# Joining the k and v products of two units, two output slots, and another order of the last stores, in a linear-attention and ELU-MLP kernel

## The chip, the core and the metric

The kernel runs on one core of one Trainium2 chip. It is one launch, and its time is the device time of that core in microseconds. A time given for a kernel is the median of several executions; a profile is one more execution, recorded by the hardware profiler. The engines of the core run their own lists of instructions and wait for one another through semaphores: TensorE (PE, with PEld for its weight loads), VectorE (DVE), ScalarE (ACT), GpSimd (POOL) and SyncE (SP). SP, ACT and POOL can also issue DMA transfers.

## The reference

Per head, q is normalised by a softmax over its 64 features, k by a softmax over the sequence. The product of k and v is a 64x64 matrix per head; q times that matrix is the attention output. Rows of 512 features (8 heads) then go through two dense layers with an ELU between.

```python
def _attn_ref(q, k, v):                       # 8 batches, 8 heads, 576 rows, 64 features
    q_s = softmax(q, axis=-1)
    k_s = softmax(k, axis=2)
    kv = np.einsum('bhsd,bhse->bhde', k_s, v)
    return np.einsum('bhsd,bhde->bhse', q_s, kv)

def _moe_ref(x, w_in, w_out):                 # x 4608x512, w_in 512x2048, w_out 2048x512
    h = x @ w_in
    g = np.where(h > 0.0, h, np.exp(np.minimum(h, 0.0)) - 1.0)
    return g @ w_out
```

(The softmaxes are written out in the reference; they are shortened here.)

## The kernel before

**Attention.** A unit is half of the heads of one batch element, so there are 16 units, two per batch element, numbered 0 to 15. For a unit, q and k are loaded as 128x1152 tiles (`QR`, `KR`) and v as `VR`. `stage1` takes the exponential of q and k on ScalarE (L397, L427 for units 0 and 1, whose q goes in two halves; L401), casts v to bf16 with a column of ones behind it (`VB`, L414 and L417), sums q's exponentials (L429), takes reciprocals (L432) and scales q (`QS`, L440). q is transposed by TensorE for units 0 to 3 (`tp`, L464, copied out at L471 and L474 into `qsT`), and by a transposing DMA from SP for the others (`turn`, L480, widened at L490 or L492).

`kv_mm` (L520) forms the product of k and v: 36 matmuls on 64x64 quarters of the array, 65 columns each, because the column of ones gives the sum of k's exponentials as well. `m` (L529, L533) is VectorE's scaling of that product into `MBLK`. `ao_mm` (L551) and, for units 0 and 1, `ao_parts` (L563) multiply the transposed q by `MBLK`: the attention output, two matmuls of up to 512 columns. `xt` (L585, L588) copies it into `XT`, the ring of rows for the dense layers.

A TensorE group is what `side` (L495) makes: several of these parts issued as one step that owns both halves of one accumulation tile. From unit 4 on the tile is always the same one (`AB`, two banks). A unit's attention output comes in two groups (part 0 and part 1). `batch(b)` (L1010) emits, for the units n = 2b and n+1, the q work and four such groups, and hangs the k/v products of the next batch's units on them: that of unit n+2 on part 0 of unit n+1, that of unit n+3 on its part 1. Those of units 4 and 5 are groups of their own.

The v cast has two tiles, but `VB1` lies over a region that is needed later, so `vb` (L366) uses it for units 1 and 3 only; from unit 4 on all casts go to the one tile `VB0`, and a cast waits until the last product has read it.

**Dense layers.** The 4608 rows are 9 blocks of 512, j = 0 to 8. For each block and each of 8 groups g, `hg_mm` (L636) makes 256 hidden features with 8 matmuls of 512 columns. `hg` follows with ScalarE's exponential (L652, into `ESB`), a second ScalarE step (L672) or a VectorE one (L680), and VectorE's combination into `GR` (L675, L682).

Blocks 0 and 1 go through the second layer plainly (`out_mm`, L697; `out_store`, L715). From block 2 on, `pair` (L819) computes two row tiles of 128 rows at once with seven products of half matrices instead of eight, on sums and differences of `GR` that GpSimd makes (`sums` and `late`, L797) and on combinations of w_out made once (`combos`, L768). A pair has four steps. Its four quarters live in two banks, H[0] to H[3]. ScalarE copies a quarter out (`copy`, L871), VectorE adds others on (`dve`, L866), and the results are in two row tiles: X (halves XL, XR) and Y. Y is complete in the third step, X in the fourth. `store` (L722) sends a row tile out as two DMAs of 64 rows, which L730 issues. Blocks 2 to 5 do a quarter of the second layer plainly within the pair (`std`, L858); blocks 6 to 8 (`WHOLE` and up) do all of it with half matrices and are called full.

X and Y of the pairs are slots `OSB0` to `OSB2`: X alternates between slots 0 and 2 (`self.pairs`), Y is always slot 1; the very last pair puts Y into `ESB0`. A slot can be written again only when the DMAs that read it have landed.

**Order.** Every operation is an entry that `Sched.add` records, with what it reads (R), writes (W), or holds exclusively (X); from this `emit` derives the semaphore waits. In which order an engine runs its entries is written out by hand: `ORDER` holds for each engine the list of entry numbers. The second argument of `add` is an assumed duration. It has no part in the order on an engine; it places the entries of all engines in one sequence for emission and sets how many filler matmuls (L948, on a unit matrix) `fill` puts into TensorE's early waits.

Entries of the start that the lists name: 22 and 38 are the exponentials of k of units 0 and 1; 25 and 29 those of q's halves of unit 0, 41 and 45 of unit 1; 23 and 39 ScalarE's v casts; 34 and 36 copies of the transposed q of unit 0; 37 and 60 the k/v products of units 0 and 1; 44 a scaling of q of unit 1 and 52 its five transposes; 49 to 51 the scaling of unit 0's product; 56 and 57 the attention output of unit 0, 58 and 59 its copies; 64 and 65 that of unit 1; 78 and on the hidden-layer matmuls of block 0.

## Time and profile before

| | us |
|---|---|
| median of three executions | 297.68 (297.46 to 297.81) |
| profiled execution, its own time | 297.21 |
| span of the profiled execution | 295.4 |
| exponentials of the hidden layer, ScalarE L652, 72 of them | 73.8 busy |
| matmuls of the hidden layer, L636, 576 of them | 142.8 busy |
| mean clock granted to TensorE, share of full | 0.998 |

The span runs from the first to the last recorded instruction; 1.8 us of the time lie outside it. Busy time of an engine counts each moment once. A row of the timeline gives start, length, engine, line of the kernel, operation, output and input, the number of instructions merged into the row, and, in brackets, how long the engine had stood idle before and what ended that. A merged row of matmuls is as long as from its first start to its last end, and as matmuls overlap, distances between starts say more than lengths. DMA rows are the issue on a queue; the transfer lands later.

### The profile page before, as it was taken

The numbers are of one execution on the slowest core, as the hardware profiler recorded it, in microseconds if no ns is written. First come the engines' busy times: TensorE is split into PE (matmuls) and PEld (weight loads), VectorE is DVE, ScalarE is ACT, GpSimd is POOL, SyncE is SP. The second block draws the span as 40 slices with busy tenths as digits, with TensorE's granted clock in tenths as the row PEclk, the third lists the DMA queues.
The fourth block names the chain that finished last, engine by engine and source line by source line (L and its number), as shares of the span: only waits on it lengthen the run. The fifth ranks groups of instructions, "written<-read, shape, count | busy, mean of one in ns | idle before, by whom it ended". The sixth has DMA issues, their size and how long they took to land.

```text
span 295.4 us, 5358 instructions
## 1 busy us (share of the span) xinstructions
PE 284.8 (96%) x2129; PEld 242.6 (82%) x2129; DVE 176.8 (60%) x326; ACT 210.9 (71%) x249; POOL 221.1 (75%) x216
## 2 busy tenths in 40 slices
PE   2999999999999999999999999999999999999993
PEld 0588777778888889888888888888889998988993
DVE  3849925786644667566656756755445366365653
ACT  5758838979998797986887596875874576666610
POOL 2990365343689998998798778799679967899870
PEclk9999999999999999999999999999999999999999
DMA  7999998899795544767849481404203110301315
GB/s 267 400 363 390 387 389 323 216 276 338 206 277 140 145 155 84 243 106 272 240 120 277 132 244 31 93 2 93 57 0 71 38 36 2 71 13 26 71 36 144
DMA packets 36473, 50.03 MB, mean 169 GB/s; under 512 B 16352, under 2 KB 18144, under 8 KB 36448
## 3 DMA queue, kind: packets, MB, share of 16 engines
q1 hardware_dynamic: 29760, 34.09, 41.4%
q0 software_dynamic: 6528, 15.47, 17.4%
q8 instruction: 17, 0.28, 0.4%
q10 hardware_dynamic: 160, 0.13, 0.2%
q14 instruction: 8, 0.07, 0.1%
HBM read 36.70 MB, written 9.44 MB: 156 GB/s over the span
## 4 chain that ended last, share of the span: by engine, by line
PE 91%; POOL 2%; ACT 2%; DVE 1%; DMA 1%; issue 0%; POOLq 0%
PE PS L636 44%; PE PS L845 24%; PE PS L697 9%; PE PS L858 5%; PE PS L551 3%; PE PS L520 2%; POOL GR L797 2%; PE PS L948 2%; DMA QR<-in_q_dram 1%; PE PS L464 1%; DVE GR L675 1%; DVE OSB L866 1%; PE PS L563 0%; ACT qsT L471 0%; ACT ESB L672 0%
## 5 line engine op out<-in xcount | busy, mean ns | idle before, releaser
L636 PE MATMUL PS<-XT,W 128*128 128x512 f32 x576 | 142.8, 392 | 0.0
L636 PEld LDWEIGHTS PS<-XT,W 128*128 128x128 f32 x576 | 104.7, 188 | 20.6 <-ACT OSBX L715 0.4
L675 DVE SCALAR_TENSOR_TENSOR GR<-PS,ESB 128x512 fp32r<-128x512 f32 (+1 forms) x124 | 87.4, 706 | 54.4 <-ACT ESB L672 52.4
L652 ACT ACTIVATE ESB<-PS 128x1024 f32<-128x1024 f32 x72 | 73.8, 1027 | 44.9 <-PE PS L636 43.8
L672 ACT ACTIVATE ESB<-ESB 128x1024 f32<-128x1024 f32 x64 | 67.9, 1060 | 1.4
L797 POOL TENSOR_TENSOR GR<-GR 128x512 fp32r<-128x512 f32 (+1 forms) x65 | 62.9, 980 | 5.1 <-PE PS L845 3.9
L866 DVE TENSOR_TENSOR OSB<-OSB,PS 128x256 f32<-128x256 f32 x83 | 34.5, 416 | 35.2 <-PE PS L845 34.5
L845 PE MATMUL PS<-W,GR 128*128 128x256 f32 x288 | 46.0, 284 | 0.3 <-POOL GR L797 0.3
L440 POOL TENSOR_TENSOR QS<-QR,RZQ 128x1152 f16<-128x1152 f32 (+1 forms) x16 | 30.3, 1895 | 20.3 <-DVE RZQ L432 19.7
L845 PE MATMUL PS<-TB,GR 128*128 128x256 f32 x288 | 43.5, 283 | 0.0
L845 PEld LDWEIGHTS PS<-W,GR 128*128 128x128 f32 x288 | 40.7, 191 | 2.5 <-POOL GR L797 0.5
L845 PEld LDWEIGHTS PS<-TB,GR 128*128 128x128 f32 x288 | 39.7, 190 | 1.7
L797 POOL TENSOR_TENSOR SB<-GR 128x256 fp32r<-128x256 f32 (+1 forms) x31 | 30.1, 975 | 13.5 <-DVE GR L675 11.8
L697 PE MATMUL PS<-W,GR 128*128 128x512 f32 x128 | 33.1, 398 | 0.0
L797 POOL TENSOR_TENSOR GR<-SB,GR 128x256 fp32r<-128x256 f32 (+1 forms) x31 | 29.9, 980 | 2.7 <-PE PS L845 2.2
L417 POOL CAST VB<-VR 128x1152 bf16<-128x1152 f32 (+1 forms) x16 | 18.0, 1122 | 14.5 <-DMA VR<-in_v_dram 9.8
L697 PEld LDWEIGHTS PS<-W,GR 128*128 128x128 f32 x128 | 23.2, 188 | 4.9 <-DMA W<-in_moe_w_out_dram 0.3
L585 ACT ACTIVATE XT<-PS 128x512 fp32r<-128x512 f32 (+6 forms) x32 | 19.2, 605 | 9.9 <-PE PS L551 5.8
L429 DVE TENSOR_REDUCE ZQ<-QR 128x18 f32<-128x1152 f32 (+2 forms) x18 | 21.7, 1206 | 6.0 <-ACT QR L427 4.2
L401 ACT ACTIVATE KR<-KR 128x1152 bf16<-128x1152 f32 x16 | 18.4, 1159 | 1.2 <-DMA KR<-in_k_dram 1.2
L858 PE MATMUL PS<-W,GR 128*128 128x512 f32 x64 | 17.6, 396 | 0.0
L871 ACT ACTIVATE OSB<-PS 128x256 f32<-128x256 f32 x27 | 10.1, 380 | 9.8 <-PE PS L845 7.5
(59 smaller groups left out, 223.0 us busy)
## 6 DMA issues: line engine op xcount, KB each, us to landing
out_dram<-OSB SPq DMA_DIRECT2D x60, 128.0 KB, 2.4
QR<-in_q_dram SPq DMA_DIRECT2D x12, 576.0 KB, 4.8
KR<-in_k_dram SPq DMA_DIRECT2D x12, 576.0 KB, 5.1
VR<-in_v_dram SPq DMA_DIRECT2D x12, 576.0 KB, 5.4
W<-in_moe_w_out_dram POOLq DMA_DIRECT2D x4, 1024.0 KB, 16.8
QR<-in_q_dram POOLq DMA_DIRECT2D x4, 576.0 KB, 9.3
KR<-in_k_dram POOLq DMA_DIRECT2D x4, 576.0 KB, 13.0
VR<-in_v_dram POOLq DMA_DIRECT2D x4, 576.0 KB, 12.9
```

The source lines that it names most:

```text
L429: S.add("dve", t_dve(m), lambda e, qp=qp, zp=zp: e.tensor_reduce(zp, qp, AX.X, ALU.add), key - 3, R=[f"qR{i}{x}" for x in xs], W=[f"ZQ{i}{ ...
L440: lambda e, qp=q[:, :, a:b, :], rz=rz, dst=qs[:, :, a:b, :]: e.tensor_tensor(dst, qp, rz, ALU.mult),
L585: S.add("act", t_act((h1 - h0) * n_, True), lambda e, dst=dst, src=src: e.activation(dst, src, AF.Copy), key, W=W, X=X)
L636: last = e.matmul(P[:, t * 512:(t + 1) * 512], self.W1[:, kc, tt * 128:(tt + 1) * 128], self.XT[:, kc, rc:rc + BLK], start=(kc == 0), stop ...
L652: S.add("act", t_act(1024, True), lambda e: e.activation(esb[:, :], self.PS[ps][:, :], AF.Exp), key, W=[f"E{i}"], X=banks)
L672: S.add("act", t_act(1024, False), lambda e: e.activation(esb[:, :], esb[:, :], AF.Relu, bias=1.0, scale=-1.0), key, X=[f"E{i}"])
L675: S.add("dve", t_dve(512 if j else 1024), lambda e, u=u: e.scalar_tensor_tensor(*(x[:, :, u, :] if j else x for x in (gt, P)), 0.0, ev[:, ...
L697: last = e.matmul(dst, self.tile(jb, jj, ts), self.W2[:, jj, c0:c1], start=(jj == 0), stop=(jj == 15))
L797: lambda e: e.tensor_tensor(dst, a, b, op), key, R=R, W=W, X=X, after=after)
L845: last = e.matmul(dst, a[i][:, y_, :], b[i][:, y_, :], start=start and i == 0 and y_ == 0, stop=stop and i == len(grps) - 1 and y_ == z - ...
L858: last = e.matmul(self.bank(bk), self.tile(j, jj, 2 * ts + p), self.W2[:, jj, :], start=False, stop=stop and jj == jj1 - 1, skip_group_che ...
L866: S.add("dve", t_dve(256), lambda e: e.tensor_tensor(dst, a, b, ALU.add), key, R=R, W=W, X=X, after=after)
```

## The change

- The k/v products of units n+2 and n+3 are parts of one group: both hang on part 1 of unit n+1, in neighbouring columns. Units 4 and 5 have one group for both (`kv2`). Assumed durations 615 and 350 become 505 and 305.
- The bf16 tile of v alternates for all units; `VB1` has memory of its own.
- Two slots `OSB0` and `OSB1` are allocated, and three more (`OSB2` to `OSB4`) lie over the raw q and k tiles. Pairs of blocks 2 to 5 use slots 0 and 1, X and Y changing places from pair to pair. Full pairs use slots 0 and 1 for the first pair of a block and 2 and 3 for the second.
- In the last pair the right half of the last row tile goes into slot 4, is finished in the third step, before the last matmuls, and is stored then; the left half is finished and stored after them.
- Of the last block's second row tile, the second half of the rows goes out on ScalarE's queue (the condition names block 8 and row tile 1).
- All five lists of `ORDER` are replaced. With one entry fewer from the group of units 4 and 5 on, entry numbers there stand one lower than before.

The core of the diff, with those pieces of the lists that are spoken of:

```diff
 ORDER = {
     "pe": (
-        "35 54 33 37 52 56 57 60 78 80 79 64 65 83 81 84 87 82 85 88 86 89 99 103 110 133 121 107 "
+        "35 54 33 37 57 56 52 60 78 80 79 64 65 82 81 84 87 85 88 83 86 89 99 103 110 121 107 133 "
...
-        "999 1021 1022 1055 1027 1028 1056 1023 1029 1057 1052 1010 1053 1031 1037 1054 1079 1080 "
-        "1038 1081 1039 1043 1113 1064 1084 1090 1085 1117 1091 1086 1073 1092 1114 1118 1094 "
+        "1056 991 1017 1051 1052 1009 1053 1078 1030 1026 1079 1020 1083 1021 1042 1022 1027 1028 "
+        "1080 1084 1063 1036 1037 1089 1090 1091 1112 1085 1038 1072 1113 1093 1099 1100 1116 "
...
-        "1294 1288 1289 1295 1290 1267 1268 1269 1282 1283 1284 1304 1305 1298 1299 1300 1306 "
-        "1309 1310 1311 1315 1316 1317 "),
+        "1294 1266 1267 1268 1281 1282 1287 1283 1288 1289 1303 1304 1305 1297 1298 1299 1311 "
+        "1312 1313 1317 1318 1319 "),
     "act": (
-        "3 29 25 45 41 22 23 36 34 38 39 58 53 66 90 93 94 96 100 101 104 111 112 114 122 108 134 "
+        "3 29 45 25 22 41 23 36 38 34 39 58 53 66 90 93 94 96 100 101 104 111 112 122 108 137 114 "
...
     "dve": (
-        "4 2 5 6 0 7 30 31 46 47 26 27 42 28 43 44 49 50 51 59 55 61 62 63 67 91 92 95 97 98 102 "
+        "4 2 5 6 0 7 30 31 46 47 26 27 28 42 43 49 50 51 44 59 55 61 62 63 67 91 92 95 97 98 102 "
...
     "sp": (
...
-        "420 333 424 489 556 530 546 531 432 438 557 545 567 439 623 572 622 638 568 637 586 679 "
+        "418 419 489 488 530 529 555 438 544 545 556 437 428 622 621 566 567 637 573 636 678 703 "
...
-        "1172 1234 1235 1286 1287 1303 1302 1313 1314 1319 1322 "),
+        "1233 1234 1218 1286 1285 1308 1301 1302 1315 1321 "),
...
-        self.OSB = [a(f"OSB{i}", [128, 512], F32) for i in range(3)]
+        self.OSB = [a(f"OSB{i}", [128, 512], F32) for i in range(2)]
         rbase = nc.sbuf_base
...
+        self.OSB += [nc.alloc_sbuf_tensor_at(f"OSB{i}", [128, 512], F32, offset=rbase + 5120 + 2048 * i)
+                     for i in (2, 3, 4)]
...
-        self.VB = [a("VB0", [128, 2, CH, D + 1], BF16),
-                   at("VB1", [128, 2, CH, D + 1], BF16, offset=tbase + 8192)]
+        self.VB = [a(f"VB{i}", [128, 2, CH, D + 1], BF16) for i in range(2)]
...
     def vb(n):
-        return 1 if n in (1, 3) else 0
+        return n % 2
...
-        return 615 if at == self.KV else 350, [f"kR{i}", f"VB{vb}", f"VB{vb}x", f"VB{vb}y", f"VBone{vb}"], mm
+        return 505 if at == self.KV else 305, [f"kR{i}", f"VB{vb}", f"VB{vb}x", f"VB{vb}y", f"VBone{vb}"], mm
...
-            q = "act" if x and c1 - c0 == 256 else "sp"
+            q = "act" if x and (c1 - c0 == 256 or (jb, ts) == (NBLK - 1, 1)) else "sp"
...
-        x, y = (2 * (self.pairs % 2), 1)
+        if full:
+            x, y, over = 2 * ts, 2 * ts + 1, []
+            if (j, ts) == (WHOLE, 1):
+                over = ["qR10", "qR11"]
+        else:
+            x, y, over = self.pairs % 2, 1 - self.pairs % 2, []
         self.pairs += 1
-        X, Y, over = self.OSB[x], self.OSB[y], []
-        if end:
-            Y, y, over = self.ESB[0], "e", ["E0"]
+        X, Y = self.OSB[x], self.OSB[y]
+        VR, late = self.OSB[4][:, 256:], ["qR10", "qR11", "kR1"]
...
             mms(1, H[1], A21, T3, h, 1)
-            dve(XR, XL, H[1], [f"O{x}L"], [f"O{x}R"], [f"b{b1}"], done)
+            if end:
+                dve(VR, XL, H[1], [f"O{x}L"], ["O4R"] + late, [f"b{b1}"])
+                dve(VR, VR, H[3], [], [], ["O4R", f"b{b1}"])
+                self.store(j, 2 * ts + 1, self.OSB[4], 4, key, 256, 512)
+            else:
+                dve(XR, XL, H[1], [f"O{x}L"], [f"O{x}R"], [f"b{b1}"], done)
...
             mms(1, H[1], A22, T4, g, 2, stop=True)
             dve(XL, XL, H[1], [], [], [f"O{x}L", f"b{b1}"])
+            if not full:
+                dve(XR, XR, H[3], [], [], [f"O{x}R", f"b{b1}"])
             if end:
                 self.store(j, 2 * ts + 1, X, x, key, 0, 256)
-            if not full or end:
-                dve(XR, XR, H[3], [], [], [f"O{x}R", f"b{b1}"])
-            if end:
-                self.store(j, 2 * ts + 1, X, x, key, 256, 512)
             else:
                 self.store(j, 2 * ts + 1, X, x, key)
...
-                cols = [(m, self.KV + D + 1) for m in kvn]
+                cols = [(m, self.KV + (D + 1) * y) for y, m in enumerate(kvn)]
...
+        def kv2(n):
+            def go():
+                cols = [(n, self.KV), (n + 1, self.KV + D + 1)]
+                self.side(AB, due(n), *[self.kv_mm(m, AB, y) for m, y in cols])
+                for m, y in cols:
+                    self.m(m, AB, due(m) - 4, y)
+            return n, go
...
-                yield from (first(n), kv(n), loads(("v", n + 1), ("q", n + 2)), first(n + 1, "k"),
-                            loads(("v", n + 2)), wide(n), kv(n + 1), loads(("k", n + 2), ("k", n + 3)))
+                yield from (first(n), loads(("v", n + 1), ("q", n + 2)), first(n + 1, "k"),
+                            loads(("v", n + 2)), wide(n), kv2(n), loads(("k", n + 2), ("k", n + 3)))
...
-            yield from (ao(n, 0), ao(n, 1), first(n + 1, "q"), loads(("q", n + 3)), wide(n + 1))
-            more = n + 2 < NU
-            if more:
-                yield from (first(n + 2, "k"), loads(("v", n + 3)))
-            yield ao(n + 1, 0, (n + 2,) if more else ())
-            if more:
-                yield from (first(n + 3, "k"), loads(("v", n + 4)))
-            yield from (ao(n + 1, 1, (n + 3,) if more else ()), loads(("k", n + 4), ("k", n + 5)))
+            yield from (ao(n, 0), ao(n, 1), first(n + 1, "q"), loads(("q", n + 3)), wide(n + 1),
+                        ao(n + 1, 0))
+            nxt = (n + 2, n + 3) if n + 2 < NU else ()
+            for m in nxt:
+                yield from (first(m, "k"), loads(("v", m + 1)))
+            yield from (ao(n + 1, 1, nxt), loads(("k", n + 4), ("k", n + 5)))
```

More of the change, by code (lines that the diff above doesn't have):

```diff
@@ L709, in out_store @@
         else:
-            i = self.oslot % len(self.OSB)
+            i = self.oslot % 2
             self.oslot += 1
@@ L760, in combos @@
         else:
-            early = [f"Ox{i}{x}" for i in range(4) for x in "LR"] + ["VB1", "VB1x", "VB1y", "VBone1"]
+            early = [f"Ox{i}{x}" for i in range(4) for x in "LR"]
         old, hi = [f"B{grp}"], grp == 2
@@ L877, in first @@
             mms(0, H[0], A11, B11, m, None, True)
-            copy(XL, H[0], [f"O{x}L"], b0)
+            copy(XL, H[0], [f"O{x}L"] + over, b0)
             mms(1, H[3], S1, T1, N1, 3, True)
```

114 rows, old and new, of the table ORDER are left out of this document.

## The prediction

> **What bounds the kernel now.** I read the page first: engines, then the chain of waits that ended last.
>
> ```profile
> span 295.4 us, 5358 instructions
> PE 284.8 (96%) x2129; PEld 242.6 (82%) x2129; DVE 176.8 (60%) x326; ACT 210.9 (71%) x249; POOL 221.1 (75%) x216
> PE 91%; POOL 2%; ACT 2%; DVE 1%; DMA 1%; issue 0%; POOLq 0%
> ```
>
> TensorE is the bound: 91% of the chain is matmuls, and its sequence hardly stops between 14 us and 291 us. So time can be won in three places only: fewer nanoseconds of TensorE work, an earlier first block, a shorter tail behind the last matmul. The change touches all three. A busy PE is not a PE at its peak, so I then looked at starts in the matmul timeline, where lost nanoseconds show as intervals.
>
> **The k/v product groups.** The timeline of TensorE around one attention output group without a k/v product, and one with it:
>
> ```profile
> 113.09 0.87 PE L845 MATMUL PS<-TB,GR 128*128 128x256 f32 x6
> 113.80 0.45 PE L551 MATMUL PS<-qsT,MBLK 128*128 128x320 f32 x2
> 114.09 0.64 PE L845 MATMUL PS<-W,GR 128*128 128x256 f32 x4
> ...
> 126.18 0.45 PE L551 MATMUL PS<-qsT,MBLK 128*128 128x320 f32 x2
> 126.56 0.48 PE L520 MATMUL PS<-VB,KR 64*64 64x65 bf16 x36
> 126.98 0.98 PE L845 MATMUL PS<-W,GR 128*128 128x256 f32 x6
> 127.79 1.09 PE L858 MATMUL PS<-W,GR 128*128 128x512 f32 x4
> ```
>
> Without the product: six 256-column matmuls last 113.80-113.09 = 0.71 us from start to start, and two of 320 columns 114.09-113.80 = 0.29. With it, the same two and the same six span 127.79-126.18 = 1.61. So the product costs 1.61-0.71-0.29 = 0.61 us of TensorE. How much of that is work? A view of one line's instructions gives the length of one of them:
>
> ```profile
> L520 PE MATMUL PS<-VB,KR x576: 187/191/215, 10.9 to 194.5; 64*64 64x65 bf16 x192
> ```
>
> The row at 126.56 spans 0.48 with its last matmul's 0.19, so the 36 start within 0.29 us. Work 0.29-0.30; the other 0.31 is paid at the two edges: 126.56-126.18 = 0.38 instead of 0.29 on entry (0.09), 0.42-0.29 = 0.13 from the last product to the next start, and 127.79-126.98 = 0.81 instead of 0.71 behind it (0.10). A second product in the same group has no edges of its own. 576/36 = 16 groups; the change joins units 4 to 15 in six pairs, so six pairs of edges go: 6 x 0.31 = **-1.9 us**. The bound on the small side: should the last 0.10 belong to something else, 6 x 0.21 = -1.3. The work itself is the same. I take -1.9, since the row measures all three parts. All six lie before 195 us with TensorE work behind them, so everything later shifts with them.
>
> What could stop that shift is GpSimd, which prepares operands for the products:
>
> ```profile
> 120.00:140.00 20.00, 20.00 (x185) 17.51 (x184) 12.66 (x28) 15.87 (x19) 18.73 (x17) 1.00 0.73 211
> ...
> 252.04 0.75 POOL L797 TENSOR_TENSOR SB<-GR 128x256 fp32r<-128x256 f32 x1 [0.83 <-DVE GR L675]
> ```
>
> (The first is a row by stretches; after TensorE, weight load, VectorE and ScalarE comes POOL with 18.73.) It still rests 1.27 us in those 20, and at 252 us it again waits for work that TensorE releases. 1.9 us spread over 140 us fits in. The v casts no longer wait for the one bf16 buffer, as they now alternate; I cost that at nothing, it lies on GpSimd. What is added behind a joined group is the second unit's scaling on VectorE, which holds the bank longer:
>
> ```profile
> 128.03 0.17 DVE L529 RECIPROCAL RZK<-PS 128x2 f32<-128x2 f32 x1 [0.69 <-ACT XT L585]
> 130.42 0.61 DVE L533 TENSOR_TENSOR MBLK<-PS,RZK 64x128 fp32r<-64x128 f32 x2
> ...
> 132.69 0.40 PE L551 MATMUL PS<-qsT,MBLK 128*128 128x256 f32 x2
> ```
>
> That is 0.17+0.61 = 0.8 us, and the next group on that bank came 132.69-126.18 = 6.5 us after the last one: nothing with this cover, 6 x 0.8 = 4.7 if a group stood right behind each.
>
> **The two output slots.** The pairs of blocks 2 to 5 now alternate two slots, so that a pair's first copy goes into the slot from which the last pair's first row tile is stored. Three views (VectorE, SP, ScalarE) of one such turnover, and the page's row on stores:
>
> ```profile
> 125.87 0.87 DVE L866 TENSOR_TENSOR OSB<-OSB,PS 128x256 f32<-128x256 f32 x2
> ...
> 128.09 1.28 SPq L480 DMA_TRANSPOSE QT<-QS  x1
> 129.41 2.72 SPq L730 DMA_DIRECT2D out_dram<-OSB  x3
> ...
> 128.94 0.38 ACT L871 ACTIVATE OSB<-PS 128x256 f32<-128x256 f32 x1
> ...
> out_dram<-OSB SPq DMA_DIRECT2D x60, 128.0 KB, 2.4
> ```
>
> The row tile is complete at 126.3, yet its stores stand behind a transposing DMA and go out from 129.41 on. The next pair's copy runs at 128.94. In the old order of instructions two slots would make this copy wait until about 134 (second store near 131.5 plus 2.4 to landing). In the new lists SP has these two stores ahead of that transpose (489 488 530 529 555). Then: issues 126.3 to 127.5, landing 2.4 later than the second's start, 126.9+2.4 = 129.3; the copy waits 0.4. Behind it on ScalarE stands an exponential of the next block, and TensorE needs the same bank for its next quarter. There are seven such turnovers. ScalarE rests 29% of the span, which hides most of it; 7 x 0.4 = 2.8 would be the price without cover, 0 with full cover. By the row below, where the three-slot ring waited 0.2 us once in the whole run, I am nearer to the small end: **+0.4**, ends 0 and +2.8 (the upper one is a rival).
>
> ```profile
> ACT OSB L871 <- DMA out_dram<-OSB: 0.2, 1, 0.2
> ```
>
> **The start.** The lists also change the first 16 us:
>
> ```profile
> 6.05 1.26 ACT L427 ACTIVATE QR<-QR 128x512 f32<-128x512 f32 x2 [0.23 <-DMA QR<-in_q_dram]
> 8.21 1.16 ACT L401 ACTIVATE KR<-KR 128x1152 bf16<-128x1152 f32 x1 [0.90 <-DMA KR<-in_k_dram]
> 9.71 0.74 ACT L414 ACTIVATE VB<-VR 128x640 bf16<-128x640 f32 x1 [0.34 <-DMA VR<-in_v_dram]
> 10.36 1.37 ACT L471 ACTIVATE qsT<-PS 128x512 fp32r<-128x512 f16 x2
> 11.42 0.45 PE L464 MATMUL PS<-ID,QS 128*128 128x128 f16 x5
> 11.62 1.16 ACT L401 ACTIVATE KR<-KR 128x1152 bf16<-128x1152 f32 x1
> 12.33 0.73 PE L563 MATMUL PS<-qsT,MBLK 128*128 128x512 f32 x2
> 13.60 0.48 PE L520 MATMUL PS<-VB,KR 64*64 64x65 bf16 x36
> 14.01 1.65 PE L636 MATMUL PS<-XT,W 128*128 128x512 f32 x6
> 15.51 0.63 PE L563 MATMUL PS<-qsT,MBLK 128*128 128x512 f32 x2
> ```
>
> ScalarE's new order is: k exponential of unit 0, last q half of unit 1 (0.63, half of the row at 6.05, where it stood before), v cast, one transposed copy, k exponential of unit 1, and only then the second transposed copy. With the rows' lengths: 8.21+1.1 = 9.3, cast from 9.95, copy 10.6 to 11.2, exponential to 12.4, second copy to 13.0. The attention output (now two matmuls at 12.33) needs that copy: it starts at 13.1, some 0.75 later. TensorE then runs it (0.7), the five transposes that stood ahead of it before (0.45), and unit 1's product (0.5): the first block begins at about 14.7 instead of 14.01. In exchange unit 1's output, which at 15.51 came some 0.1 to 0.2 behind the six matmuls, no longer waits: net +0.5. One later wait, 0.3 us of TensorE for the first part of w_out to land, takes up some:
>
> ```profile
> PEld PS L697 <- DMA W<-in_moe_w_out_dram: 0.3, 1, 0.3
> ```
>
> I take **+0.3**, ends -0.1 (if a shorter list of filler matmuls lets the chain go earlier) and +0.8.
>
> **The tail.** All engines, the last 12 us:
>
> ```profile
> 286.49 0.30 PEld L845 LDWEIGHTS PS<-W,GR 128*128 128x128 f32 x2 [0.48 <-POOL GR L797]
> 289.16 1.89 SPq L730 DMA_DIRECT2D out_dram<-ESB  x2
> 290.90 0.88 DVE L866 TENSOR_TENSOR OSB<-OSB,PS 128x256 f32<-128x256 f32 x2 [0.57 <-PE PS L845]
> 291.09 2.52 SPq L730 DMA_DIRECT2D out_dram<-OSB  x4
> 291.36 1.26 ACTq L730 DMA_DIRECT2D out_dram<-OSB  x2
> ...
> L730 SPq DMA_DIRECT2D out_dram<-OSB x6: 466/596/601, 287.5 to 293.0; - x6
> DMA to landing us min/median/max: 2.1/2.4/3.8
> ```
>
> The last matmul's result is there at 290.90, and the span ends at 295.4, 4.5 us on. The two additions take 0.88, but the end is set by SP: from 289.16 it issues six stores without a rest, 0.6 each (the first two 1.89 together, so that one took some 1.4), and its last issue starts at 293.0, landing 2.1 later. The change finishes the right quarter before the last matmuls, so one addition (0.42) is left; its store and one more half go out earlier or on ScalarE's queue. Counting SP's issues from the last full row tile on: before 2+4, after 2+2 (one half of the first pair's row tile, the last left quarter); the early right quarter's issue stands ahead of them. The last issue can then start at 290.90+0.46 = 291.36 if SP is free, or near 292.4 if that one long issue and the early one push it: gain 293.0-291.36 = 1.65 at best, 0.6 at least. Between them I take **-1.2**: two issues of 0.6 less is what the rows count.
>
> A rule speaks against the second queue. The Trainium skill, DMA: Bandwidth & Descriptors, section "Rules for kernel authors", says that two transfers to disjoint partition halves serialize even when issued from two engines, since both use the same DMA engines. By that rule the second half of the last row lands behind the first; with the 0.3 us between the least and the median landing time as its length the term would be -0.9.
>
> Ahead of it TensorE waits 0.5 us for GpSimd's last subtraction. The new list puts four more 256-column matmuls behind that point (38 instead of 34, 4 x 0.12 = +0.47). GpSimd's long last stretch, from the row at 252.04 on, is released by a hidden-layer block that is now listed six such matmuls earlier (-0.7), which takes off about as much. I set this at **0**, ends -0.35 and +0.47.
>
> **Sum.** -1.9+0.4+0.3-1.2+0 = -2.4. The profiled execution took 297.21 us (295.4 span and 1.8 around it), 0.5 less than the median of the runs, 297.68; taken from its own time that is 294.8, and on the median's footing 297.68-2.4 = **295.3 us**.
>
> **Rivals.**
> *Slower: the store behind the ring.* If a load, 0.5 to 0.6 on SP, still goes ahead of the stores at each turnover, the copy waits longer than its cover and the bank stalls TensorE: 7 x 0.6 = 4.2 in place of 0.4 gives 295.3+3.8 = 299.1. It decides from 0.4 us of TensorE per turnover on, where 2.8 eats the gain. For it: the old order would have lost 5 us at the turnover shown. Against it: the new list moves exactly those stores. Chance 0.09.
> *The edges go and nothing is won.* GpSimd is the true pace from 80 to 200 us and TensorE's 1.9 becomes waiting for it: 297.2. For it: 18.73 of 20 busy. Against: the chain of waits gives POOL 2%. Chance 0.09.
> *The tail stays.* The long issue (1.4 of the 1.89) falls on the new queue order too and the last store starts near 293: tail -0.2, so 296.3. For it: nothing in the rows says what made it long. Against: two issues fewer stand behind it. Chance 0.10.
> The forecast: 0.72, with its own range 293.9 to 296.6.
>
> **How the numbers follow.** All ends at their best give -1.9-0.1-1.65-0.35 = -4.0, thus 293.7; with -1.3, +0.8, -0.6, +0.47 and the ring at +0.4 it is -0.2, thus 297.5. The range 293.8 to 297.4 holds the forecast, the tail's rival and most of GpSimd's; the slower rival and the extremes are left out. A measurement tells 0.2%, 0.6 us, from no change (297.1 to 298.3). Faster: 0.72 of the forecast less 0.01, 0.10 of the tail's, 0.04 of GpSimd's: 0.85. Within: 0.05 of GpSimd's and 0.01. Slower: 0.09.
>
> **What would show it.** Right: ten groups of product matmuls instead of sixteen, six of them with 72, whose edges cost 0.31 as those of one product do now; last SP issue within 1.5 us of the last matmul; end under 3.5 us behind it. Wrong: ScalarE's quarter copies waiting for stores for more than 2 us in total, TensorE waiting for POOL between 80 and 200 us, a first block of hidden-layer matmuls later than 14.9, or TensorE's last block arriving before GpSimd by more than 1 us. A time above 298.3 with whole edges saved would mean that the ring is the cause.

## The result, and the profile after

| | before | after |
|---|---|---|
| median, us (lowest to highest of 5) | 297.68 (297.06 to 298.65) | 296.21 (295.94 to 296.37) |
| profiled execution, its own time | 297.21 | 295.94 |
| its span | 295.4 | 293.8 |
| ratio of after to before, 95% interval | | 0.9947 (0.9926 to 0.9968) |

The change makes the kernel faster by 1.5 us, and the prediction had said 2.4 (295.3, range 293.8 to 297.4). The page of the changed kernel:

```profile
span 293.8 us, 5345 instructions
PE 282.6 (96%) x2130; PEld 241.9 (82%) x2130; DVE 177.3 (60%) x326; ACT 211.0 (72%) x249; POOL 220.2 (75%) x216
PE 90%; DVE 3%; POOL 2%; DMA 2%; ACT 1%; POOLq 0%; issue 0%; SPq 0%
```

TensorE still bounds the kernel. Its busy time fell by 2.2 us; the span fell by 1.6. To see where the rest went, I follow single matmuls through both traces: the 1st, the 65th and the 569th of the 576 hidden-layer matmuls start at 14.01, 47.93 and 273.26 us before. After, they start at 15.03, 48.88 and 272.78. So the new kernel loses 0.95 us up to 48 us (predicted 0.3), gains 0.95+0.48 = 1.43 from there to 273 us (predicted 1.9-0.4 = 1.5), and the end of the span gains 1.57-0.48 = 1.1 more behind that (predicted 1.2). The start is what differs.

**Middle.** The timeline of TensorE around a joined group:

```profile
128.69 0.64 PE L850 MATMUL PS<-TB,GR 128*128 128x256 f32 x4
129.17 0.40 PE L552 MATMUL PS<-qsT,MBLK 128*128 128x256 f32 x2
129.50 0.78 PE L521 MATMUL PS<-VB,KR 64*64 64x65 bf16 x72
130.21 0.74 PE L850 MATMUL PS<-W,GR 128*128 128x256 f32 x4
130.79 0.88 PE L850 MATMUL PS<-W,SB 128*128 128x256 f32 x6
```

There are 72 product matmuls in one row, 130.21-129.50 = 0.71 us long, of which 0.13 is the exit; entry (0.09) and the 0.10 behind are there once. All six joined groups read 0.90 to 0.94 in this way, where one product alone had cost 0.61: 2 x 0.61-0.91 = 0.31, as predicted.

**Start.** The same kernel from 12 to 15 us, all engines, and the wait that follows at 27 us:

```profile
12.45 1.73 DVE L441 TENSOR_TENSOR QS<-QR,RZQ 128x640 f16<-128x640 f32 x1
12.54 0.73 ACT L415 ACTIVATE VB<-VR 128x640 bf16<-128x640 f32 x1
12.62 0.87 POOL L418 CAST VB<-VR 128x512 bf16<-128x512 f32 x1
12.69 0.73 PE L564 MATMUL PS<-qsT,MBLK 128*128 128x512 f32 x2 [0.19 <-ACT qsT L472]
...
14.23 0.45 PE L465 MATMUL PS<-ID,QS 128*128 128x128 f16 x5 [0.80 <-DVE QS L441]
14.61 0.48 PE L521 MATMUL PS<-VB,KR 64*64 64x65 bf16 x36
...
15.03 1.66 PE L637 MATMUL PS<-XT,W 128*128 128x512 f32 x6
```

```profile
25.71 1.22 DVE L676 SCALAR_TENSOR_TENSOR GR<-PS,ESB 128x1024 fp32r<-128x1024 f32 x1 [0.28 <-ACT ESB L673]
26.85 0.68 DVE L681 TENSOR_SCALAR ESB<-ESB 128x1024 f32<-128x1024 f32 x1
...
26.98 0.50 PE L637 MATMUL PS<-XT,W 128*128 128x512 f32 x1 [0.30 <-DVE GR L676]
```

VectorE's scaling of unit 1's q (entry 44, L441) now stands behind the scaling of unit 0's product. Here it ran beside GpSimd's cast of v and took 1.73 us, and the transposes, the product of unit 1 and the first block waited. At 25 to 27 us TensorE stops again, for 0.45 us, until VectorE's product (L676) has freed a bank. The kernel before had no stop there; its twelve matmuls follow one another within 0.24 us:

```profile
24.61 2.88 PE L636 MATMUL PS<-XT,W 128*128 128x512 f32 x12
```

**Ring and tail.** From the views of ScalarE's waits, of SP's stores and of the last microseconds:

```profile
ACT OSB L876 <- DMA out_dram<-OSB: 4.7, 4, 2.7
```

```profile
L731 SPq DMA_DIRECT2D out_dram<-OSB x63: 466/592/1626, 81.1 to 290.7; - x63
```

```profile
286.34 4.97 SPq L731 DMA_DIRECT2D out_dram<-OSB  x7
...
288.09 2.08 PE L850 MATMUL PS<-TB,GR 128*128 128x256 f32 x16
288.25 2.90 ACTq L731 DMA_DIRECT2D out_dram<-OSB  x3
...
290.20 0.42 DVE L871 TENSOR_TENSOR OSB<-OSB,PS 128x256 f32<-128x256 f32 x1 [0.53 <-PE PS L850]
```

Four quarter copies waited 4.7 us for stores (0.2 before), yet TensorE shows no wait for them. One addition stands at the end; SP's last issue starts at 290.7, right behind it, and 0.8 us after the start of the last matmul (289.89); before, it started at 293.0, 2.4 us after (290.58). The end followed by less: from 4.8 us behind that matmul to 3.95.

### The profile page after: what moved, and what is told of

Its sections match the earlier page's. It is cut to its first block, busy times and chain, and to the rows that moved or that the text cites. A ratio compares the mean times of both kernels' runs of the same rounds, so it can differ in the third digit from the quotient of the medians.

```text
span 293.8 us, 5345 instructions
## 1 busy us (share of the span) xinstructions
PE 282.6 (96%) x2130; PEld 241.9 (82%) x2130; DVE 177.3 (60%) x326; ACT 211.0 (72%) x249; POOL 220.2 (75%) x216
## 4 chain that ended last, share of the span: by engine, by line
PE 90%; DVE 3%; POOL 2%; DMA 2%; ACT 1%; POOLq 0%; issue 0%; SPq 0%
PE PS L637 43%; PE PS L850 26%; PE PS L698 10%; PE PS L863 5%; PE PS L552 3%; PE PS L521 2%; DMA QR<-in_q_dram 2%; POOL GR L798 1%; DVE GR L676 1%; ACT ESB L653 1%; DVE QS L441 1%; PE PS L465 1%; POOL W L379 0%; POOLq L285 0%; DVE GR L683 0%; ACT ESB L673 0%
## 5 line engine op out<-in xcount | busy, mean ns | idle before, releaser
L676 DVE SCALAR_TENSOR_TENSOR GR<-PS,ESB 128x512 fp32r<-128x512 f32 (+1 forms) x124 | 87.4, 705 | 57.2 <-ACT ESB L673 52.4
L798 POOL TENSOR_TENSOR GR<-GR 128x256 fp32r<-128x256 f32 (+1 forms) x65 | 62.3, 977 | 6.0 <-PE PS L850 5.2
L441 POOL TENSOR_TENSOR QS<-QR,RZQ 128x1152 f16<-128x1152 f32 (+1 forms) x16 | 30.3, 1894 | 26.1 <-DVE RZQ L433 24.8
L850 PE MATMUL PS<-W,GR 128*128 128x256 f32 x288 | 45.1, 284 | 0.1
L698 PE MATMUL PS<-W,GR 128*128 128x512 f32 x128 | 32.7, 395 | 0.0
L863 PE MATMUL PS<-W,GR 128*128 128x512 f32 x64 | 17.3, 391 | 0.0
```

The lines of the kernel that those rows point to most:

```text
L441: lambda e, qp=q[:, :, a:b, :], rz=rz, dst=qs[:, :, a:b, :]: e.tensor_tensor(dst, qp, rz, ALU.mult),
L676: S.add("dve", t_dve(512 if j else 1024), lambda e, u=u: e.scalar_tensor_tensor(*(x[:, :, u, :] if j else x for x in (gt, P)), 0.0, ev[:, ...
L698: last = e.matmul(dst, self.tile(jb, jj, ts), self.W2[:, jj, c0:c1], start=(jj == 0), stop=(jj == 15))
L798: lambda e: e.tensor_tensor(dst, a, b, op), key, R=R, W=W, X=X, after=after)
L850: last = e.matmul(dst, a[i][:, y_, :], b[i][:, y_, :], start=start and i == 0 and y_ == 0, stop=stop and i == len(grps) - 1 and y_ == z - ...
L863: last = e.matmul(self.bank(bk), self.tile(j, jj, 2 * ts + p), self.W2[:, jj, :], start=False, stop=stop and jj == jj1 - 1, skip_group_che ...
```

## The experiments

Entry numbers are those of the changed lists. The table gives what all executions with a profile say of the three stretches, as starts of the matmuls named above minus the start in the profile of the kernel before. Starts and span of a line are one execution; the ratio rests on 5 to 12 executions of that kernel.

| execution | 1st (14.01) | 65th (47.93) | 569th (273.26) | span (295.4) | ratio of times, 95% interval |
|---|---|---|---|---|---|
| changed kernel | +1.01 | +0.95 | -0.49 | 293.8 | 0.9947 (0.9926 to 0.9968) |
| e5_after, the same | +0.31 | +0.60 | -0.52 | 293.8 | 0.9947 (0.9928 to 0.9966) |
| e7_tail_queue | +0.62 | +0.93 | -0.51 | 294.1 | 0.9947 (0.9930 to 0.9964) |
| e8_tail_right | +0.40 | +0.24 | -1.05 | 293.5 | 0.9955 (0.9938 to 0.9973) |
| e12_tail_old | +0.33 | +0.03 | -1.37 | 293.5 | 0.9947 (0.9926 to 0.9967) |
| e4_edges | +0.40 | +0.05 | +0.06 | 294.4 | 1.0010 (0.9993 to 1.0027) |
| e11_store_late | +0.50 | +0.13 | +14.30 | 308.7 | 1.0436 (1.0412 to 1.0460) |
| e1_head_old | -0.15 | +0.01 | -1.43 | 292.9 | 0.9936 (0.9923 to 0.9949) |
| e6_head_long | -0.13 | -0.01 | -1.46 | 292.9 | 0.9924 (0.9903 to 0.9946) |
| e10_old_start_w_in | +0.04 | +0.15 | -0.97 | 294.1 | 0.9951 (0.9939 to 0.9964) |
| e2_head_dve | +0.93 | +1.23 | +0.24 | 294.6 | 0.9965 (0.9950 to 0.9980) |
| e3_head_act | -0.01 | +0.20 | -1.25 | 293.1 | 0.9959 (0.9940 to 0.9978) |
| e9_w_in_first | +0.73 | +0.98 | -0.41 | 293.9 | 0.9947 (0.9935 to 0.9960) |

The kernel before took 297.1 to 297.3 us beside these runs, so 0.001 is 0.3 us.

**e4_edges: the edges paid again.**

```diff
-                parts = [self.ao_mm(n, x, ps)] + [self.kv_mm(m, ps, y) for m, y in cols]
+                parts = [self.kv_mm(m, ps, y) for m, y in cols[:1]] + [self.ao_mm(n, x, ps)] + [
+                    self.kv_mm(m, ps, y) for m, y in cols[1:]]
```

> The changed kernel with the attention output's two matmuls between the two k/v products of a joined group instead of ahead of both, so that the edges into and out of the 64x64 matmuls are paid twice again in the groups that hold an attention output (five of the six joined groups); the same instructions, buffers and order otherwise. Theory (edges are TensorE time and what they save arrives in full): 5 x 0.31 = 1.55 us more than the changed kernel, 297.7, and groups of 36 that cost 0.6 each. Rival (GpSimd is the pace between 80 and 200 us): the edges come back in the timeline, but less than 0.5 us of it in the time, 296.2 to 296.7. Entry alone (0.09 of the 0.31) would give 296.7.

```profile
128.54 0.40 PE L850 MATMUL PS<-TB,GR 128*128 128x256 f32 x2
128.87 0.48 PE L521 MATMUL PS<-VB,KR 64*64 64x65 bf16 x36
129.28 0.51 PE L552 MATMUL PS<-qsT,MBLK 128*128 128x256 f32 x2
129.72 0.48 PE L521 MATMUL PS<-VB,KR 64*64 64x65 bf16 x36
130.13 0.73 PE L850 MATMUL PS<-W,GR 128*128 128x256 f32 x4
```

128.87-128.54 = 0.33 for two matmuls that take 0.24: the entry is there twice, and 129.72-129.28 = 0.44 for the attention output that took 0.33 shows the step between. The 569th matmul comes 1.43 us later than in e12_tail_old, which had the same start (+0.03 against +0.05). That is 0.29 for each of the five groups. Against the eleven other executions of the table (e11_store_late left out), the stretch from the 65th to the 569th matmul is 1.00 to 1.46 us longer, 1.33 on the mean, or 0.27 per group. It reaches the time: 1.0010-0.9947 = 0.0063, or 1.9 us; by the medians against e5_after, 296.97-295.79 = 1.2. GpSimd as the pace, which allowed less than 0.5, is out.

**e1_head_old, e2_head_dve, e3_head_act: the order of the start.** The first takes all four lists of the start back, the other two one each.

```diff
     "dve": (
-        "4 2 5 6 0 7 30 31 46 47 26 27 28 42 43 49 50 51 44 59 ...
+        "4 2 5 6 0 7 30 31 46 47 26 27 42 28 43 44 49 50 51 59 ...
     "act": (
-        "3 29 45 25 22 41 23 36 38 34 39 58 ...
+        "3 29 25 45 41 22 23 36 34 38 39 58 ...
     "pe": (
-        "35 54 33 37 57 56 52 60 78 80 79 64 65 82 81 84 87 85 88 83 86 ...
+        "35 54 33 37 52 56 57 60 78 80 79 64 65 83 81 84 87 82 85 88 86 ...
     "gp": (
-        "1 32 48 14 17 24 15 16 ...
+        "1 32 48 14 15 24 16 17 ...
```

> The changed kernel (296.2 us) with the order of the kernel before for the first instructions of TensorE, ScalarE, VectorE and GpSimd (up to the first hidden-layer blocks); everything later as changed. Theory (the new order of the start costs more than the 0.3 us that was predicted: the first hidden-layer matmul came at 15.03 instead of 14.01, and a stall of 0.46 us at 26.3 us follows from it): first block near 14.0 to 14.3, the time 0.7 to 1.3 below, thus 294.9 to 295.5. Rival (the late start is the spread of landing times, 0.32 us for the first q tile in that one profile, the order itself costs the predicted 0.3): 295.9 to 296.2, with a first block at 14.6 or later.

> Only VectorE's first instructions go back to the old order: unit 1's scaling of q stands ahead of unit 0's k/v scaling again. Theory A (VectorE's place for that one operation makes the late start, since the transposes of unit 1 wait for it until 14.22): the transposes are free from about 13.0 on, attention output first at about 13.3 since unit 0's scaling is now 0.8 later, first block near 14.5: 0.4 to 0.6 below the changed kernel, 295.6 to 295.8. Theory B (what was predicted: ScalarE's second transposed copy behind the k exponential is what is late): no gain or a loss, 296.2 to 296.6.

> Only ScalarE's first instructions go back to the old order (both transposed copies of unit 0 ahead of unit 1's k exponential). Theory B (ScalarE's order is what delays the start, as predicted): attention output near 12.4 instead of 12.69 and first block 0.5 earlier, 295.7. Theory A (VectorE's late scaling of unit 1 is): the first block stays within 0.2 of 15.0 and the time within 0.3 of 296.2.

With all four, the first block is at 13.86 and TensorE stands at +0.01 at 48 us: the 0.95 is gone. But the stop at 25 us, now 0.77 long, had eaten the 0.15 that it was ahead. The span is 0.9 us shorter than in the first profile, as expected, but the time is lower by only 0.9947-0.9936 = 0.0011, or 0.3 us, where 0.7 to 1.3 were expected, and the intervals overlap. ScalarE's list alone (e3) brings the first block to 14.00, as before the change; VectorE's alone (e2) leaves it at 14.95. That is theory B, the mechanism of the prediction. It holds over the whole table: the four executions with ScalarE's old list (e1, e3, e6, e10) have the first block at 13.86 to 14.05, the nine with its new list at 14.32 to 15.03. By the ratio, neither e2 nor e3 takes less time than the changed kernel.

What theory A had seen is a second thing on top. In the first profile VectorE's scaling took 1.73; in e5_after, the same kernel, the same two operations read:

```profile
12.34 0.83 DVE L441 TENSOR_TENSOR QS<-QR,RZQ 128x640 f16<-128x640 f32 x1
12.62 1.03 POOL L418 CAST VB<-VR 128x512 bf16<-128x512 f32 x1
```

Here VectorE was through in 0.83, and the cast took 1.03 and ended 0.48 behind it. In the first profile the cast was through at 13.49, and VectorE ended 0.69 behind that. One of the two waits for the other. Which one, the recorded starts do not tell. The same pair in e9_w_in_first, and in e11_store_late:

```profile
12.16 1.74 DVE L441 TENSOR_TENSOR QS<-QR,RZQ 128x640 f16<-128x640 f32 x1
...
12.34 0.88 POOL L418 CAST VB<-VR 128x512 bf16<-128x512 f32 x1
```

```profile
12.66 0.83 DVE L441 TENSOR_TENSOR QS<-QR,RZQ 128x640 f16<-128x640 f32 x1
...
12.82 1.16 POOL L418 CAST VB<-VR 128x512 bf16<-128x512 f32 x1
```

VectorE started 0.17 us ahead of the cast in the first profile and 0.18 in e9, and waited; it started 0.28 ahead in e5_after and 0.15 (unrounded) in e11, and did not. What decides is open. Where VectorE waited, the first block came at 15.03 and 14.75; in the six other executions with that start it came at 14.32 to 14.63.

The Trainium skill, SBUF — State Buffer, section "Who interferes with whom", says that a VectorE instruction with two inputs in SBUF contends with a GpSimd instruction that reads SBUF, over a port pair that it calls an exclusive lock. The traces agree. The Trainium skill says there too that the order of issue decides who waits; the recorded starts, which put VectorE first in all four, do not show that order.

**e6_head_long, e9_w_in_first, e10_old_start_w_in: the stop at 25 us.** e6 takes the old order of the first 38 us on four engines; e9 swaps two issues of GpSimd; e10 is e1 with that swap.

```diff
     "gp": (
-        "1 32 48 14 17 24 15 16 18 40 19 20 68 21 73 ...
+        "1 32 48 14 17 24 15 16 18 40 19 20 21 68 73 ...
```

> The changed kernel with the old order of the first 38 us on TensorE, ScalarE, VectorE and GpSimd: the start as in the run with the old order of the start, and also the second unit's blocks behind it, where that run stopped for 0.77 us at 25.2 us and the kernel before did not stop at all. Theory (the stall came from joining an old start to the new order of the blocks that follow): no stall at 25 us, first block near 13.9, 0.5 to 0.9 below the run with the old start (0.9936 of before), ratio 0.991, 294.5. Rival (TensorE there waits for the landing of the next part of w_in, which has its own time near 26.2; an earlier start only makes the wait longer): the stall comes back somewhere before 40 us, ratio 0.9936.

> The changed kernel with two of GpSimd's DMA issues in the old order: the last part of w_in ahead of the next q load, instead of behind it. In the changed kernel that part landed at 26.1 and 26.6 us (24.6 before), and TensorE stood still at 25.6 to 26.9 us for 0.46 and 0.91. Theory (that landing is what TensorE waits for there, so it undoes any earlier start): the part lands near 24.6, no wait for it; where the first block is at 14.4 or earlier the stall goes and 0.5 to 0.9 us with it, with a first block near 15.0 the 0.46 that VectorE's product sets stays: ratio 0.9917 to 0.9935. Rival (VectorE's chain of products sets the restart at 26.9, the landing was only near it): stall of 0.4 or more remains, ratio within 0.001 of 0.9947.

> The run with the old order of the start (ratio 0.9936, a stall of 0.77 us until the last part of w_in had landed at 26.02), with the last part of w_in ahead of the next q load besides. Theory (start and landing each hide the other; with both repaired all of it arrives): landing near 24.6, no stall of more than 0.2 us at 25 us, 0.6 to 0.8 below: ratio 0.991, 294.4 on a mark of 297.1. Rival (the next landing or VectorE takes over): a stall of 0.3 to 0.8 comes back between 21 and 45 us as in the run with the old order of the first 38 us, ratio 0.9924 to 0.9936.

In e9 the last part of w_in landed at 24.6, as planned, and nothing was won:

```profile
25.47 1.23 DVE L676 SCALAR_TENSOR_TENSOR GR<-PS,ESB 128x1024 fp32r<-128x1024 f32 x1 [0.28 <-ACT ESB L673]
26.62 0.69 DVE L681 TENSOR_SCALAR ESB<-ESB 128x1024 f32<-128x1024 f32 x1
26.75 0.74 PE L637 MATMUL PS<-XT,W 128*128 128x512 f32 x2 [0.36 <-DVE GR L676]
```

The rival holds. In all executions with that stop TensorE goes on 0.13 to 0.14 us behind the later of two events: the end of VectorE's product, read at the start of its next operation (26.85 in the changed kernel, 26.62 in e9, 26.12 in e10), or that landing (26.60 in e5_after, 26.18 in e3). In the new order of the blocks they lie 0.01 to 0.75 us apart, except where e9 and e10 bring the landing forward, so taking one away uncovers the other. The old order of the blocks (e6) has no stop there, and a stop of 0.33 us at 21.5 us instead, where another part of w_in lands at 21.9. All three runs with the old start stand between -0.01 and +0.15 at 48 us.

e10 shows another collision of VectorE and GpSimd, at 62 us, and e5_after the same place without it:

```profile
61.81 1.15 POOL L418 CAST VB<-VR 128x1152 bf16<-128x1152 f32 x1 [1.70 <-DMA VR<-in_v_dram]
...
62.49 1.02 DVE L681 TENSOR_SCALAR ESB<-ESB 128x1024 f32<-128x1024 f32 x1 [0.98 <-ACT ESB L653]
```

```profile
62.17 1.15 POOL L418 CAST VB<-VR 128x1152 bf16<-128x1152 f32 x1 [1.07 <-PE PS L637]
...
63.25 0.69 DVE L681 TENSOR_SCALAR ESB<-ESB 128x1024 f32<-128x1024 f32 x1 [0.90 <-ACT ESB L653]
```

0.33 us more on VectorE became a stop of 0.38 us of TensorE at 64.6 us; e11_store_late stopped for 0.63 in the same way. With e10's late end (4.7 us behind the last matmul, where two of SP's last issues took 1.19 and 0.87) this makes about 1.1 of the 1.2 us by which this execution's span is longer than that of e1. All five spans of e10, 293.5 to 294.1, lie above the mean of e1's, 293.25; whether the others had the same two causes no trace shows.

**e5_after: the changed kernel once more.**

> The changed kernel once more, unaltered, as the mark for the other runs beside it and to see what its start does in another execution. All theories: ratio to the kernel before 0.9947 within its interval of 0.9926 to 0.9968; the first hidden-layer block between 14.4 and 15.1, which the three runs with whole or part of its start order have shown (15.03, 14.95 and 14.41).

The ratio came out the same. The first block was at 14.32, 0.7 us earlier than in the first profile, but TensorE waited 0.91 us at 25.6 for w_in, and the 569th matmul stands at -0.52 instead of -0.49.

**e7_tail_queue, e8_tail_right, e12_tail_old: the tail.** e7 sends half of the last left quarter over SP again, e8 finishes the last right quarter behind the left one again, e12 undoes both; the lists follow.

```diff
-            q = "act" if x and (c1 - c0 == 256 or (jb, ts) == (NBLK - 1, 1)) else "sp"
+            q = "act" if x and c1 - c0 == 256 else "sp"
...
-            if end:
-                dve(VR, XL, H[1], [f"O{x}L"], ["O4R"] + late, [f"b{b1}"])
-                dve(VR, VR, H[3], [], [], ["O4R", f"b{b1}"])
-                self.store(j, 2 * ts + 1, self.OSB[4], 4, key, 256, 512)
-            else:
-                dve(XR, XL, H[1], [f"O{x}L"], [f"O{x}R"], [f"b{b1}"], done)
+            dve(XR, XL, H[1], [f"O{x}L"], [f"O{x}R"], [f"b{b1}"], done)
...
             if end:
                 self.store(j, 2 * ts + 1, X, x, key, 0, 256)
+                dve(XR, XR, H[3], [], [], [f"O{x}R", f"b{b1}"])
+                self.store(j, 2 * ts + 1, X, x, key, 256, 512)
```

In e7 the condition on ScalarE is dropped and the one entry goes to SP's list.

> The changed kernel with one of the last row tile's stores, the other half of the last left quarter, issued by SP behind its first half instead of by ScalarE; all else as changed. Theory (SP's issues, 0.6 each, set the end of the tail): the last issue starts 0.6 later and the end comes 0.6 later, from 3.95 to 4.5 us behind the last matmul's start; in the time +0.6. Rival (the rule that both halves share the DMA engines, so that two queues gain nothing): 0, 3.9 to 4.0 us.

> The changed kernel with the last right quarter finished behind the last left one again, as before the change, and stored from the slot of its pair; the last stores stay on two queues. Theory (the early quarter takes one addition of 0.42 and its store out of the end): the end comes 0.5 to 0.9 later behind the last matmul, 4.5 to 4.8 us instead of 3.95, time +0.5 to +0.9. Rival (the second queue alone made the gain): 3.9 to 4.1 us and no change in the time.

> The changed kernel with both parts of the tail undone: the last right quarter finished behind the last left one, and only the two quarter stores of the second half on ScalarE's queue, as before the change. Undone singly, the parts moved the end by 0.3 (second queue: from 3.95 to 4.23 us behind the last matmul's start) and 0 (right quarter: 3.96, with 0.25 us more of TensorE's waiting ahead of it). Theory (either part alone keeps SP nearly free, only both together bring back the four issues in a row of 0.6 that ended the kernel before): the last SP issue starts 2.2 to 2.5 us behind the last matmul's start as before (2.43; changed 0.78), the end 4.5 to 4.8 behind, time +0.6 to +1.1: ratio 0.9967 to 0.9984. Rival (the parts add up, and the landings, not the issues, set the end): end 4.2 to 4.3, time +0.3 to +0.5: ratio 0.9957 to 0.9964.

| | last matmul's start | last SP issue behind it | last landing behind it | end of span behind it | end of span behind the 569th |
|---|---|---|---|---|---|
| before | 290.58 | 2.43 | 4.52 | 4.83 | 22.15 |
| changed kernel | 289.89 | 0.78 | 3.35 | 3.95 | 21.06 |
| e7, one queue | 289.88 | 1.43 | 3.68 | 4.22 | 21.35 |
| e8, right quarter last | 289.57 | 1.28 | 3.65 | 3.96 | 21.32 |
| e12, both | 289.28 | 1.66 | 3.88 | 4.19 | 21.58 |

The rows of e12 that show the end:

```profile
285.99 5.56 SPq L731 DMA_DIRECT2D out_dram<-OSB  x7
...
287.42 1.38 DVE L871 TENSOR_TENSOR OSB<-OSB,PS 128x256 f32<-128x256 f32 x3 [0.85 <-PE PS L850]
...
289.60 0.87 DVE L871 TENSOR_TENSOR OSB<-OSB,PS 128x256 f32<-128x256 f32 x2 [0.80 <-PE PS L850]
290.05 1.20 ACTq L731 DMA_DIRECT2D out_dram<-OSB  x2
```

Each part, undone, costs 0.3 us of landing, both cost 0.53, and of SP's 1.65 us that the change had won back, 0.88 are lost. The parts add up, as e12's rival had it, and e7's cost lies between the 0.6 of its theory and the 0 of its rival. The last column counts from a matmul that stands ahead of all that was altered: there the parts cost 0.29, 0.26 and 0.52, while the nine executions with the changed tail lie within 21.04 to 21.13 (e10, with its long issues, at 21.78). None of the three shows in the time, nor in the spans: over all their executions these are 293.7, 293.8 and 293.8 on the mean, against 294.0 for twelve of the changed kernel. In single executions the stretches ahead differ by more than the tail is worth. With both undone the end lies at 4.2, not at 4.8 (21.58 against 22.15): the missing 0.6 is near what the one long issue of the kernel before (1.38 instead of 0.6) may have cost, and no issue of e12 between 285 us and the end is longer than 0.61. e10 had such issues under the changed order. What makes them long is open, and so is whether the kernel before has one in every execution.

**e11_store_late: the order behind the ring.** At six turnovers SP's stores of a pair's first row tile go behind what follows them.

```diff
     "sp": (
-        473 474 425 418 419 489 488 530 529 555 438 ... 622 621 566 567 ... 678 703 677 585 ... 767 766 714 586 ... 822 823 715
+        425 418 473 474 419 489 488 555 438 530 529 ... 566 567 622 621 ... 703 585 678 677 ... 714 586 767 766 ... 715 822 823
```

> The changed kernel with SP's order altered at six turnovers of the two output slots: the stores of a pair's first row tile go out behind the two loads or transposing DMAs that follow them (one at one turnover), 1.2 to 1.9 us later each; the same DMAs otherwise. Theory (ScalarE's rest covers the wait of the next pair's quarter copies, so the two slots cost TensorE next to nothing, 0 to 0.4 in the changed kernel): the copies wait 5 us or more longer in total, TensorE loses less than 1 us, ratio 0.995 to 0.998. Rival (the ring has no cover left and each late store counts): 6 x 1.2 to 1.9 = 7 to 11 us more, ratio 1.02 to 1.03.

```profile
112.93 1.30 SPq L481 DMA_TRANSPOSE QT<-QS  x1
114.28 1.23 SPq L731 DMA_DIRECT2D out_dram<-OSB  x2
...
117.29 0.39 ACT L876 ACTIVATE OSB<-PS 128x256 f32<-128x256 f32 x1 [5.08 <-DMA out_dram<-OSB]
```

```profile
PE PS L850 <- ACT OSB L876: 9.8, 2, 5.4
```

Both theories missed, since the delay was wrong: at two turnovers what now goes first is itself waiting (the transposing DMA for its data; at the second, behind 133 us, a load of k as well). At the first of them the stores left at 114.28 instead of 108.77, not 1.9 later but 5.5. There TensorE stopped for 4.4 and 5.4 us. At the other four turnovers the later stores cost TensorE nothing, though the copies waited 17.6 us in total instead of 4.7. So both are seen: cover at four places, and too little at two, where the transposing DMA must not go first. A view by stretches shows what came after the two stops (the number after the busy times is the granted clock):

```profile
113.00:117.70 4.70, 0.32 (x2) 0.00 (x0) 0.95 (x2) 0.41 (x2) 4.70 (x5) 0.91 0.69 145
117.70:124.00 6.30, 6.27 (x22) 5.50 (x23) 1.38 (x2) 4.68 (x5) 2.21 (x3) 0.52 0.21 81
124.00:130.00 6.00, 6.00 (x35) 5.24 (x34) 4.64 (x9) 4.85 (x8) 2.21 (x3) 1.00 0.19 44
143.10:147.30 4.20, 4.20 (x17) 3.81 (x17) 2.33 (x7) 1.09 (x2) 1.48 (x2) 0.50 1.01 365
```

TensorE ran at half its clock (0.52) for 6.3 us behind the first stop, and again (0.50) for 4.2 us behind the second. Against the changed kernel's first profile TensorE went from 0.24 us ahead at 111 us to 14.77 behind at 143 us. Of these 15.0 us 9.8 are the two waits, and 6.3 x 0.48 + 4.2 x 0.50 = 5.1 is that clock. The Trainium skill, TensorE: Matmul & The Clock Gate, section "What's actually happening", says that a window of about 3.4 us of idleness halves the clock; both stops here were longer, and the trace agrees.

## Why the prediction was right, and where it was off

- **Edges, -1.9: right.** 0.31 per pair in the timeline; undoing five of them cost 0.27 each of TensorE on the mean (0.20 to 0.29), which makes -1.6 for six, and it arrived in the time.
- **Ring, +0.4: small, as predicted, though the warning sign showed.** The copies waited 4.7 us in total, over the 2 us that the prediction had named as a sign of error, and one of them 2.7 where 0.4 was set for each. But this lay in ScalarE's rest: no wait of TensorE is put down to it. From 48 to 273 us TensorE gained 1.43 in the first profile, and 1.32 on the mean of the eleven executions; with -1.6 for the edges, 0.3 is left for the ring and everything else. The slower rival is out for the order as changed, and e11 shows that its mechanism is real where a store is late.
- **Start, +0.3 from a first block at 14.7: the mechanism was right, the size too small.** The step named ScalarE's order, and e3 confirms it. What failed is "in exchange unit 1's output no longer waits" and "takes up some": they gave back less than was set. And VectorE's own new order was not priced: entry 44 moved to where the cast of v runs. In the first profile the start cost 0.95 at 48 us, and its first block (15.03) showed the sign of error "later than 14.9". Over the seven executions with that start (e9, with another order of loads, left out) the first block lies at 14.32 to 15.03, mean 14.5, and the cost at 48 us at 0.03 to 0.95, mean 0.42. Spans give more: 293.2 on the mean of the twelve executions with the old start (e1, e6), 294.0 for twelve of the changed kernel. By these the new order of the early instructions costs 0.8, the end of the prediction's range for this term.
- **Tail, -1.2: the size was near (-1.1 against this profile), partly by luck.** The last SP issue moved by 2.43-0.78 = 1.65, the best case given. But the last landing moved only 1.17, as it came 2.56 us after its issue instead of 2.09, and the end only 0.88, as it came 0.60 behind that landing instead of 0.31. Behind the last matmul's result, as the prediction counts, the end lies 293.84-290.20 = 3.6 us, over the 3.5 that it had named as a sign of being right. The two edits themselves are worth 0.52, as e12 shows; the other 0.57 has no shown cause, and the one profile of the kernel before cannot tell whether it is there in every execution. The -0.9 by the rule of the Trainium skill (DMA: Bandwidth & Descriptors, "Rules for kernel authors") is nearer to what the end moved than the -1.2. That is partly chance too: the two last landings stand 0.17 apart (293.06 and 293.23), not 0.3.
- **Waiting for GpSimd in the tail, 0:** it fell from 0.44 to 0.23 us, inside its bounds.

The prediction's term by term sum against the first profile: start 0.65 worse, middle 0.1, tail 0.1, together 0.8 of the 0.83 by which the span missed (-1.57 instead of -2.4). Another 0.3 lies outside the span: 295.94-293.8 = 2.1 instead of 1.8. Over its 12 executions the changed kernel has 2.0 there, the kernel before 1.8; why is open. Taken by what the experiments gave (edges -1.6, rest of the middle +0.3, start +0.4, tail -0.5), the sum is -1.4, near the 1.5 measured. This agreement is loose: the sum leaves out the unexplained 0.57 of the tail and the 0.2 outside the span, and with 0.8 for the start it would be -1.0. The time is near that of the rival "the tail stays" (296.3), but not for its reason.

By the ratios, no version tried beats the changed kernel beyond doubt. The old start with the rest of the change (e1, e6) is lowest, 0.9936 and 0.9924, with intervals that overlap that of the changed kernel. Its spans, 292.7 to 293.8 in twelve executions against 293.2 to 294.6, speak for it; it would be the next thing to build on.

## What to carry to other kernels

Small matmuls in another tile shape are best put in one run, since each visit cost about 0.3 us of TensorE here. An earlier start is worth only what the next wait leaves of it: look for the second event that lies within tenths of the first before a reorder is priced. A moved VectorE operation with two inputs in SBUF has the price of what GpSimd does at its new place, not of its own row.

## What was not expected of the hardware

- VectorE and GpSimd hold each other up: the same scaling took 0.83 us where the cast ended 0.48 behind it, and 1.73 where it ended 0.69 behind the cast. Recorded starts 0.15 to 0.18 us apart went either way. It is one reason why the first block of one and the same kernel came at 15.03 and at 14.32.
- After stops of 4.4 and 5.4 us the granted clock was 0.52 for 6.3 us and 0.50 for 4.2 us.
- SP's issue of a store takes 0.47 to 0.6 us as a rule, up to 1.63 in the changed kernel's first profile and 3.46 in e10 (at 63 us). The cause is open, but it is not scattered: one and the same store, near 98 us, took 0.97 to 1.94 in all thirteen executions of the table.
